# Batch 0's last scores masked on DVE, masks and products joined in pairs, and a new hand-written order, in a kernel of windowed attention and a gated long convolution

## Chip, cores and metric

One core of one Trainium2 chip. The metric is the device time of a launch in microseconds, the median of several runs. Engines: PE (matrix products), DVE (element-wise), ACT (exponentials, copies, casts), POOL (here it issues loads) and SP (issues stores and small copies).

## What is computed

Four batches, eight heads of 64, 768 positions. An attention in which a query sees the 96 keys up to its own position and the first 8 keys, with a bias that falls with distance, feeds a convolution over the whole length, done in frequency space between two gates:

```
keep   = is_global | is_local
scores = where(keep, q @ k.T / 8 - slope[h] * dist, -1e9)
a      = softmax(scores)
x      = (a @ v), heads side by side          # 4 x 768 x 512
x1, x2, x3 = split(x @ w_proj)
conv   = irfft(rfft(x2) * rfft(filter))
out    = (x1 * conv * x3) @ w_out
```

## The kernel before

The work of a batch goes through two halves. **Attention:** q and k rows are turned on PE (L703) and copied to `QT` and `KT` by ACT or DVE (L321). The keys are cut in seven blocks, in three groups, the thirds (`GRP`, `c` = 0, 1, 2); for each of four head pairs and each third a step `scores` (L737) makes 128x864 scores in two PSUM banks (L755), ACT takes their exponential into `E` (L770), and the bias and the window come in as a multiplication by `mask` on DVE (L787), a table of exponentials of the scaled distance tile `dg` that ACT makes head by head (L623; `dg` is shown as `eo` in the profile). In batch 0 the masks are not ready so early: while `c < NEAR` the step is a `near` one, where PE adds the bias by two matmuls of a scaled identity with `dg` (L749), and no multiplication follows. `values` (L805, L810) multiplies with v; DVE or ACT divide by the sums (L829, L833), and PE and a copy turn the result into `xT` (L851).

**Convolution:** `gate` (L931) makes x1 and x3 from `xT` and the outer columns of the projection `w`, ACT scales x1 and DVE multiplies (`g`, L945). `butterfly` (L860) makes sums and differences of `xT` so that the length-768 transform needs smaller products: `xab`, `xcf`, then `xo` and `xs`; in batch 0 it goes in two halves (head pairs 0 and 1), later in one. `proj` (L996) multiplies them with the middle columns of `w`, `fwd` (L1162) transforms, `products` (L1175) multiplies the spectrum `X` with the filter's two parts `h1` and `h2`, `inv` (L1027) and `mixed`, `gated` (from L1105) go back, and L1089 makes the output, which ACT or DVE copy out and SP stores.

**Order.** Nothing decides at build time: `ORDER` is a text with one word for each step, its number, its engine (P, A, V, G, S) and its PSUM banks; `i2b1` is two idle matmuls in bank 1. `Plan.schedule` reads it, and each engine runs its steps in that sequence. Where a step may run on ACT or DVE, the letter decides. All loads of q, k, v, `w` and the filter stand in POOL's sequence: `w` comes in five pieces (`WL`): columns 0, 1024, 256, 1280 (256 each) and 512 (512 columns, the projection's), each with the 128-row blocks side by side. The pieces 0 and 256 feed x1, 1024 and 1280 x3.

The words that the prediction uses: a *landing* is the arrival of a load; *xs* are the last differences of the butterfly (L886, L887), *xo* its odd part (L874).

## Time and profile before

| | before |
|---|---|
| median of 3 runs | 162.05 us (161.91 to 162.38) |
| profiled execution | 162.59 us |
| its span, first to last instruction | 160.8 us |
| mean clock of PE | 0.995 |
| loaded and stored | 21.95 MB, 136 GB/s on the mean |

The span is cut in views: busy time of each engine in a stretch (windows), the same instructions grouped by line (with mean duration and the idle time before them), the timeline of one engine (start, duration, line, operation, out<-in, count; in brackets the idle time before it and what ended it), the waits by who was waited for, the chain that ended last, and the loads with their time from issue to landing. PE stands for matmuls, PEld for its weight loads. Shapes are partitions x elements. In a row of the timeline several instructions of a kind are taken together, from the start of the first to the end of the last; start to start is an instruction's pace, which is shorter than its duration where two overlap.

### The profile page before, as it was taken

The page shows a single profiled execution, that of the slowest core. Times are in us where ns is not written, and L with a number is a line of the kernel's source. Part 1 is how long each engine was busy: PE and PEld are TensorE (multiplying, and loading weights), DVE is VectorE, ACT ScalarE, POOL GpSimd, SP SyncE. Part 2 cuts the span into 40 slices and gives each one's busy share as a digit, 9 for nine tenths or more (in the row PEclk, how much of TensorE's full clock was granted, in tenths as well). Part 3 has the DMA queues.
Part 4 walks back from the last instruction along what each step waited for, and adds up shares of the span by engine and source line. Part 5 has one row for each costly group of instructions (what it writes and reads, how often), then busy time and mean ns, then how long its engine had stood idle before and what let it go on. Part 6 is the DMA issues. An engine that isn't in the chain of part 4 may idle for free.

```text
span 160.8 us, 4208 instructions
## 1 busy us (share of the span) xinstructions
PE 151.4 (94%) x1587; PEld 91.8 (57%) x1587; DVE 150.3 (93%) x354; ACT 152.1 (95%) x299; POOL 77.1 (48%) x101
## 2 busy tenths in 40 slices
PE   5884999999999999999999999999999999999990
PEld 2543348745556678655567575545766754574540
DVE  5899989998999999999999999999999999999960
ACT  7999999999999999999999999999999999999761
POOL 7999469989988998989992000000000000000000
PEclk9999999999999999999999999999999999999998
DMA  5999999999999999999999985736002000330685
GB/s 165 212 178 166 154 149 132 135 161 163 186 166 152 147 131 136 164 151 155 153 103 152 134 158 102 71 131 248 17 33 104 0 0 0 132 135 0 264 325 196
DMA packets 84956, 21.95 MB, mean 136 GB/s; under 512 B 75584, under 2 KB 81992, under 8 KB 84936
## 3 DMA queue, kind: packets, MB, share of 16 engines
q0 software_dynamic: 73040, 12.11, 102.0%
q1 hardware_dynamic: 11896, 9.57, 22.4%
q8 instruction: 12, 0.20, 0.5%
q14 instruction: 8, 0.07, 0.1%
HBM read 25.40 MB, written 6.29 MB: 197 GB/s over the span
## 4 chain that ended last, share of the span: by engine, by line
PE 71%; ACT 11%; POOL 9%; DMA 3%; issue 3%; DVE 0%; POOLq 0%
PE bank L931 22%; PE bank L996 13%; PE bank L1089 13%; PE bank L755 4%; POOL qn L346 4%; POOL kn L346 4%; DMA w<-in_moe_w_proj_dram 3%; PE bank L1027 3%; PE bank L1162 3%; PE bank L805 3%; ACT E L770 3%; PE bank L851 3%; PE bank L810 3%; PE bank L703 2%; ACT mask L623 2%
## 5 line engine op out<-in xcount | busy, mean ns | idle before, releaser
L931 PE MATMUL bank<-xT,w 128*128 128x384 f16 x256 | 48.4, 326 | 0.3 <-DMA w<-in_moe_w_proj_dram 0.3
L770 ACT ACTIVATE E<-bank 128x864 f16<-128x864 f32 x48 | 41.7, 962 | 0.2 <-PE bank L755 0.2
L931 PEld LDWEIGHTS <-w 128*128 128x128 f16 x256 | 23.5, 98 | 16.7 <-DMA w<-in_moe_w_proj_dram 1.2
L346 POOL DMA_DIRECT2D vn<-in_v_dram x28 | 25.8, 936 | 1.6 <-DMA kn<-in_k_dram 0.8
L346 POOL DMA_DIRECT2D kn<-in_k_dram x25 | 21.5, 876 | 4.4 <-DVE eo L327 2.3
L1089 PE MATMUL bank<-wo,y 128*128 128x512 f16 (+1 forms) x100 | 23.2, 371 | 0.0
L346 POOL DMA_DIRECT2D qn<-in_q_dram x25 | 21.5, 870 | 1.6 <-PE bank L1034 0.5
L787 DVE TENSOR_TENSOR E<-E,mask 128x864 f16<-128x864 f16 x36 | 20.7, 600 | 0.0
L325 ACT ACTIVATE x<-bank 128x384 f16<-128x384 f32 x32 | 17.7, 579 | 1.0 <-PE bank L931 0.9
L325 ACT ACTIVATE ot<-bank 128x512 f32<-128x512 f32 (+1 forms) x23 | 14.9, 666 | 2.2 <-PE bank L1089 2.1
L996 PE MATMUL bank<-w,xs 128*128 128x512 f16 x64 | 16.0, 379 | 0.0
L805 PEld LDWEIGHTS <-E 128*128 128x128 f16 x224 | 14.1, 97 | 2.5 <-ACT E L770 0.2
L805 PE MATMUL bank<-vn,E 128*128 128x65 f16 x224 | 15.2, 193 | 0.0
L1089 PEld LDWEIGHTS <-y 128*128 128x128 f16 x100 | 9.4, 98 | 9.9 <-DVE y L1144 0.8
L810 PE MATMUL bank<-vn,E 128*128 128x65 f16 x192 | 15.0, 193 | 0.0
L321 ACT CAST ab<-bank 128x512 f16<-128x512 f32 x24 | 14.8, 658 | 0.0
L755 PE MATMUL bank<-QT,KT 64*128 64x216 f16 (+2 forms) x224 | 14.2, 242 | 0.5 <-DVE QT L321 0.4
L945 DVE TENSOR_TENSOR g<-bank,x 128x384 f16<-128x384 f32 x24 | 13.1, 548 | 0.9 <-PE bank L755 0.6
L810 PEld LDWEIGHTS <-E 128*128 128x128 f16 x192 | 13.2, 97 | 1.1
L755 PEld LDWEIGHTS <-KT 64*128 64x128 f16 x224 | 7.8, 94 | 10.4 <-issue 9.2
L829 DVE TENSOR_TENSOR xn<-bank,rc 128x512 f16<-128x512 f32 (+1 forms) x18 | 13.5, 761 | 0.1
L321 ACT CAST X<-bank 128x1024 f16<-128x1024 f32 x12 | 13.0, 1081 | 0.3 <-PE bank L1162 0.2
(155 smaller groups left out, 325.2 us busy)
## 6 DMA issues: line engine op xcount, KB each, us to landing
out_dram<-ot SPq DMA_DIRECT2D x23, 256.0 KB
vn<-in_v_dram POOLq DMA_DIRECT2D x28, 120.0 KB, 7.5
kn<-in_k_dram POOLq DMA_DIRECT2D x16, 96.0 KB, 5.1
qn<-in_q_dram POOLq DMA_DIRECT2D x16, 96.0 KB, 5.1
w<-in_moe_w_proj_dram POOLq DMA_DIRECT2D x4, 256.0 KB, 5.7
kn<-in_k_dram POOLq DMA_DIRECT2D x7, 120.0 KB, 6.8
g<-in_moe_filter_fft_dram POOLq DMA_DIRECT2D x1, 768.0 KB, 9.5
qn<-in_q_dram POOLq DMA_DIRECT2D x6, 128.0 KB, 7.2
```

The costliest lines, as they stand in the source:

```text
L321: {"A": nc.scalar.copy, "V": nc.vector.tensor_copy, "G": nc.gpsimd.tensor_copy}[e](out, in_)
L325: self.nc.scalar.mul(out, in_, c)
L346: return self.g.op(eng, 0.57 + 0.00035 * nbytes[0] if eng == "G" else 0.5, lambda _: e.dma_start(dst, src), w=w, r=r, nbytes=nbytes, name= ...
L755: nc.tensor.matmul(bs[hh].f32()[:, off:off + w], self.KT[hs, hp, P * m:P * m + P], self.QT[hs, hp, KL * m:KL * m + w], start=(off == 0 and ...
L770: g.op("A", act(864), lambda _: nc.scalar.activation(eo, bs[0].two()[:, :, 0:432].rearrange("p h (m w) -> p h m w", m=2), Act.Exp, scale=s ...
L787: g.op("V", dve(864, 2), lambda _: nc.vector.tensor_mul(eo, eo, mk), r=[("mask", 2 * hp), ("mask", 2 * hp + 1)], w=[("E", hp, gi)], name=" ...
L805: nc.tensor.matmul(o[:, n, hh], ef[:, at:at + P], vt[:, t, 2 * hp + hh, 0:D + 1], start=first, stop=(t == 0), skip_group_check=True)
L810: nc.tensor.matmul(o[:, n, hh], ef[:, at:at + P], vt[:, t - 1, 2 * hp + hh, 0:D + 1], start=False, stop=True, skip_group_check=True)
L829: nc.vector.tensor_mul(to, o[:, :, :, 0:D], rc.to_broadcast([P, 2, 2 * nt, D]))
L931: nc.tensor.matmul(bk.f32()[:, 0:h], self.w[:, c, o + P * j:o + P * j + P], self.xT[:, c, h * s:h * s + h], start=(c == 0), stop=(c == 3))
L996: nc.tensor.matmul(bk.f32(), src[:, c], w[:, c, DM:2 * DM], start=(c == 0), stop=(c == 3))
L1089: nc.tensor.matmul(bk.f32()[:, 0:n], y[:, c, P * t:P * t + P], self.wo[:, c, cs], start=(c == 0), stop=(c == 3))
```

## The change

Six things change. **Masks:** `PAIR_M` lists all batches and thirds, so one DVE instruction masks two head pairs (128x1728) where two did (128x864): 36 become 18 in batches 1 to 3. **Batch 0's last third:** `NEAR` is 2, so its four score steps lose their two bias matmuls each, and two joined masks are added. **Butterfly:** batch 0's comes in one instead of two halves (`JOIN0`), and the two instructions of the turned differences are one, in all batches. **Products:** the two with `h1` and `h2` are one instruction of 2048 elements (`h1`, `h2` in one tile; `X` has 8 slots, the last two are the old `p3`). **`neg`,** a table that nothing used, is not made. **Order:** a new `ORDER`, with other engine letters: from DVE to ACT go the copies and fills of `dg` (`second`), the scaling of `fold`, two fills of ones and one copy of `xT`; from ACT to DVE two casts of q and k, copies of `KT` and `QT`, two scalings of x1, one part of `xn` and three copies of outputs. Counts: DVE 356 to 310, ACT 301 to 297, PE 1587 to 1580 matmuls; POOL's 106 and SP's 53 stay, in the same sequence.

The code, and the first words of the two orders:

```diff
@@ -39,51 +39,50 @@
...
-44S 3G 1V 4V 46S 31G 5V 0V 21P5 55S 2A 29A 8V 48S 16P4 7V 22A 30V 11P2 54G 17A 23V 45A i2b1 53G 24V 12A 33V 6G 18V
-25A 19V 50G 82P1 47A 13V 32V 34G 20A 80P0 38A 51G 41A 26A 198P4 14V 52G 83A 36V 92P5 56V 71G 15A 204V 58S 200V 49V
...
+44S 3G 1V 4V 46S 31G 5V 0V 21P6 55S 2A 10V 29A 48S 11P1 9V 22A 33V 54G 7V 32A i1b0 23V 16P5 53G 45V i2b0 24V 6G 17A
+18A 47V 50G 82P4 12A 19V 80P6 40A 34G 13V 25A 51G 14V 37A 20A 36V 81A 52G 191P7 43V 35V 15A 49V 71G 56V 86P3 60G 57V
...
@@ -196,11 +195,13 @@
 
 class Fused:
     PERIOD = 40.0
-    NEAR = 3
+    NEAR = 2
     SPLIT = (3,4,5)
     SUMPE = ()
     TWICE = tuple((3,j,s) for j in range(4) for s in range(2))
-    PAIR_M = ()
+    PAIR_M = tuple((b,c) for b in range(4) for c in range(3))
+    JOIN0 = True
+    DIRECT = ()
     WARM = "sin"
     PAIR_G = ()
     PAIR_AB = ()
@@ -267,17 +268,17 @@
         self.fwd = t("fwd", [P, 8, P])
         self.fold = t("fold", [P, 4, P])
         self.inv = t("inv", [P, 4, P])
-        self.neg = t("neg", [P, 2, P])
+        self.neg = t("neg", [P, 2, P]) if self.SUMPE else None
         self.uw = t("uw", [P, 4, 2, 2, P])
         self.inr = t("inr", [P, 4, P])
-        self.p3 = t("p3", [P, 2, DM])
+        self.X = t("X", [P, 8, DM])
+        self.p3 = self.X[:, 6:8]
         self.twin = self.p3.rearrange("p a b -> p (a b)")[:, 0:512].rearrange("p (s a c) -> p s a c", s=2, a=2)
-        self.h1 = t("h1", [P, 4, DM])
-        self.h2 = t("h2", [P, 4, DM])
+        self.hh = t("hh", [P, 2, 4, DM])
+        self.h1, self.h2 = self.hh[:, 0], self.hh[:, 1]
         self.gt = [t(f"g{i}", [P, 4, S]) for i in range(2)]
         self.abp = t("ab", [P, 6, DM])
         self.ab = [self.abp[:, 3 * i:3 * i + 3] for i in range(2)]
-        self.X = t("X", [P, 6, DM])
         pp = t("pp", [P, 2, 4, DM])
         self.pp = pp
         self.p1, self.p2 = ([pp[:, x, 2 * i:2 * i + 2] for i in range(2)] for x in range(2))
@@ -569,9 +570,10 @@
                 f = self.fold[64 - 64 * (s % 2):P - 64 * (s % 2), (s + 2) % 4]
                 self.times(e, f, f, c * (1 - s // 2 * 2))
         g.op("AV", {"A": 4 * act(P), "V": 4 * dve(P, 4)}, scaled, w=[("fwd", 3), "foldp"], name="foldp")
-        g.op("AV", {"A": 2 * act(P), "V": dve(2 * P, 4)}, lambda e: [self.times(
-            e, self.neg[:, n], self.inv[:, 2 - 2 * n], -1.0) for n in range(2)] if e == "A" else self.times(
-            e, self.neg[:, ::-1], self.inv[:, 0:4:2], -1.0), r=[("inv", i) for i in range(7)], w=["neg"], name="neg")
+        if self.SUMPE:
+            g.op("AV", {"A": 2 * act(P), "V": dve(2 * P, 4)}, lambda e: [self.times(
+                e, self.neg[:, n], self.inv[:, 2 - 2 * n], -1.0) for n in range(2)] if e == "A" else self.times(
+                e, self.neg[:, ::-1], self.inv[:, 0:4:2], -1.0), r=[("inv", i) for i in range(7)], w=["neg"], name="neg")
 
     def distances(self):
 
@@ -881,11 +883,16 @@
         turned = xs.rearrange("p (a b) c m -> p a b c m", a=2)[:, ::-1, :, :, 64:P]
 
         def odd(_):
+            if n == 2:
+                ahead = xs.rearrange("p (a b) c m -> p a (b c) m", a=2)[:, ::-1, :, 64:P]
+                a, c = (x.rearrange("p (a b) c m -> p a (b c) m", a=2) for x in (right, left))
+                v.tensor_sub(ahead, a, c)
+                return
             for a in range(2):
                 ins = slice(2 * a, 2 * a + 2)
                 v.tensor_sub(turned[:, a], right[:, ins], left[:, ins])
         op(dve(512 * n, 2), lambda _: v.tensor_add(xs[:, :, :, 0:64], right, left), ("xr", "xc", "xf"), "xe")
-        op(2 * dve(256 * n, 2), odd, ("xr", "xc", "xf"), "xd")
+        op(dve(1024, 2) if n == 2 else 2 * dve(256, 2), odd, ("xr", "xc", "xf"), "xd")
 
     def gates(self, b, jp, s):
         nc, g, h = self.nc, self.g, self.S // 2
@@ -932,6 +939,12 @@
                                      self.xT[:, c, h * s:h * s + h], start=(c == 0), stop=(c == 3))
             g.op("P", pe(*[h] * 4), run, acq=[bk], r=xs + [("w", o // P + j)], name="gate")
             pts.append(bk)
+        if (b, j, s) in self.DIRECT:
+            x3, ko = gt[:, j, h * s:h * s + h], ("g", b % 2, j, s)
+            g.op("V", dve(h, 1, True), lambda _: nc.vector.scalar_tensor_tensor(
+                x3, pts[0].f32()[:, 0:h], X1_SCALE, pts[1].f32()[:, 0:h], op0=Alu.mult, op1=Alu.mult),
+                use=pts, w=[ko], name="g")
+            return
         x1, key = self.x1[self.turn4 % 4], ("x1", self.turn4 % 4)
         self.turn4 += 1
         g.op("AV", self.evac(h), lambda e: self.times(e, x1, pts[0].f32()[:, 0:h], X1_SCALE),
@@ -976,7 +989,7 @@
                     for j in (2 * jp, 2 * jp + 1):
                         self.gate(b, j, c - 1)
                 self.g.bias = 0.0
-        for js in ((0,), (1,)) if b == 0 else ((0, 1),):
+        for js in ((0,), (1,)) if b == 0 and not self.JOIN0 else ((0, 1),):
             self.butterfly(js)
 
 
@@ -1177,17 +1190,20 @@
         n, m = pair[0] // 2, len(pair) // 2
         xs = X[:, pair[0]:pair[0] + 2 * m]
         if n == 2:
-            g.op("V", dve(1024, 2), lambda _: nc.vector.tensor_mul(self.p3, xs, self.h2[:, 2:4]),
-                 r=[("h", s, 2) for s in pair],
-                 w=[("X", s) for s in pair], name="prod")
-            g.op("V", dve(1024, 2), lambda _: nc.vector.tensor_mul(xs, xs, self.h1[:, 2:4]),
-                 r=[("h", s, 1) for s in pair],
-                 w=[("X", s) for s in pair], name="prod")
+            to = X[:, 4:8].rearrange("p (x s) n -> p x s n", x=2)[:, ::-1]
+            g.op("V", dve(2048, 2), lambda _: nc.vector.tensor_mul(
+                to, xs[:, None].to_broadcast([P, 2, 2, DM]), self.hh[:, ::-1, 2:4]),
+                r=[("h", s, x) for s in pair for x in (1, 2)], w=[("X", s) for s in pair], name="prod")
             return
         p1, p2 = self.pp[:, 0, pair[0]:pair[0] + 2 * m], self.pp[:, 1, pair[0]:pair[0] + 2 * m]
         rs = [("X", s) for s in pair] + [("h", s) for s in pair]
         two = lambda x: x.rearrange("p (k c) n -> p k c n", c=2)
-        for to, h, key in ((p1, self.h1, "p1"), (p2, self.h2, "p2")):
+        if m == 1:
+            g.op("V", dve(2048, 2), lambda _: nc.vector.tensor_mul(
+                self.pp[:, :, pair[0]:pair[0] + 2], xs[:, None].to_broadcast([P, 2, 2, DM]),
+                self.hh[:, :, n:n + 1].to_broadcast([P, 2, 2, DM])),
+                r=rs, w=[("p1", n), ("p2", n)], name="prod")
+        for to, h, key in ((p1, self.h1, "p1"), (p2, self.h2, "p2")) if m > 1 else ():
             g.op("V", dve(1024 * m, 2), lambda _, to=to, h=h: nc.vector.tensor_mul(
                 two(to), two(xs), h[:, n:n + m, None].to_broadcast([P, m, 2, DM])),
                 r=rs, w=[(key, n + x) for x in range(m)], name="prod")
```

Three places in the order. First ACT, from the load of its exponential table to the first exponentials of batch 0 (`mask`, `E`), before:

```order
21 L623 ACT_TABLE_LOAD
22 L623 ACTIVATE mask<-eo 128x648 x2
23 L321 COPY QT<-bank_107 128x768
24 L770 ACTIVATE E<-bank_105 128x2x2x216
25 L770 ACTIVATE E<-bank_106 128x2x2x216
26 L321 COPY KT<-bank_107 128x6x120
27 L321 COPY KT<-bank_107 128x120
28 L321 COPY KT<-bank_107 128x7x6
29 L321 COPY KT<-bank_107 128x7x2
```

and with the change:

```order
20 L625 ACT_TABLE_LOAD
21 L625 ACTIVATE mask<-eo 128x648 x5
22 L326 ACTIVATE eo<-ident 128x128
23 L322 COPY QT<-bank_104 128x768
24 L322 COPY X<-fwd 128x512
25 L326 ACTIVATE eo<-ident 128x128
26 L625 ACTIVATE mask<-eo 128x648
27 L772 ACTIVATE E<-bank_104 128x2x2x216
28 L772 ACTIVATE E<-bank_105 128x2x2x216
29 L326 ACTIVATE eo<-ident 128x128
```

Six masks instead of two stand ahead of the first exponential, and the KT copies that lay between exponentials are gone from there.

Second DVE, the last steps of batch 0's butterfly (`xab`, `xcf`, `xo`, `xs`), among products of the gates (`g`) and masks of batch 1 (`E`), before:

```order
108 L787 TENSOR_TENSOR E<-E,mask 128x2x2x216
109 L878 TENSOR_TENSOR xcf<-xab,xcf 128x2x256
110 L787 TENSOR_TENSOR E<-E,mask 128x2x2x216
111 L887 TENSOR_TENSOR xs<-xcf 128x4x2x64
112 L787 TENSOR_TENSOR E<-E,mask 128x2x2x216
113 L945 TENSOR_TENSOR g_87<-bank_107,x_94 128x384 x2
114 L787 TENSOR_TENSOR E<-E,mask 128x2x2x216
115 L886 TENSOR_TENSOR xs<-xcf 128x2x2x64 x2
116 L787 TENSOR_TENSOR E<-E,mask 128x2x2x216 x6
```

and with the change:

```order
101 L958 TENSOR_TENSOR g_85<-bank_105,x_91 128x384
102 L894 TENSOR_TENSOR xs<-xcf 128x16x64
103 L784 TENSOR_TENSOR E<-E,mask 128x4x2x216
104 L328 TENSOR_SCALAR x_91<-bank_103 128x384
105 L958 TENSOR_TENSOR g_85<-bank_103,x_91 128x384
106 L889 TENSOR_TENSOR xs<-xcf 128x2x8x64
107 L958 TENSOR_TENSOR g_85<-bank_102,x_91 128x384
108 L784 TENSOR_TENSOR E<-E,mask 128x4x2x216 x3
```

The last `xs` (L886, now L889) is one instruction, directly behind the first of the last two `g`; before, both `g` and a mask stood ahead of it. Three masks follow.

Third DVE, the end of batch 1's masks, with the return from frequency space (`eo`, `mix`, `uw`) between, before:

```order
168 L1123 TENSOR_TENSOR eo<-eo,uw 128x8x128
169 L787 TENSOR_TENSOR E<-E,mask 128x2x2x216
170 L1124 TENSOR_TENSOR eo<-mix,uw 128x8x128
171 L787 TENSOR_TENSOR E<-E,mask 128x2x2x216
172 L945 TENSOR_TENSOR g_88<-bank_108,x_94 128x384
173 L787 TENSOR_TENSOR E<-E,mask 128x2x2x216
174 L1125 TENSOR_TENSOR eo<-mix,uw 128x8x128
175 L787 TENSOR_TENSOR E<-E,mask 128x2x2x216 x2
176 L834 RECIPROCAL rc_97<-bank_107 128x8
```

and with the change:

```order
149 L958 TENSOR_TENSOR g_86<-bank_103,x_91 128x384
150 L1134 TENSOR_TENSOR mix<-eo,uw 128x1024
151 L784 TENSOR_TENSOR E<-E,mask 128x4x2x216
152 L328 TENSOR_SCALAR uw<-uw 128x8x128
153 L958 TENSOR_TENSOR g_86<-bank_103,x_91 128x384
154 L1136 TENSOR_TENSOR eo<-eo,uw 128x8x128
155 L784 TENSOR_TENSOR E<-E,mask 128x4x2x216
156 L1137 TENSOR_TENSOR eo<-mix,uw 128x8x128
157 L784 TENSOR_TENSOR E<-E,mask 128x4x2x216
158 L958 TENSOR_TENSOR g_86<-bank_105,x_91 128x384
159 L1138 TENSOR_TENSOR eo<-mix,uw 128x8x128
```

Where five masks of one head pair stood among these steps, each handed over by itself, three joined ones stand.

More of the change, by code (lines that the diff above doesn't have):

```diff
@@ new lines @@
+502V 676A 660P3 804A 744V 753P45 677P67 661A 678P 754V 518P0 755V 665A 679A 499V 619P1 519A 666P23 807V 667P 750P67
+621A 682P45 668A 683P 751V 802V 813P01 684A 515P2 814V 500V 815A 620P3 752V 808P45 622V 772P67 669V 615P3 516A
+769P01 773V 680V 617A 517S 616P2 774A 520S 506P3 770V 618V 809V 771V 756P2 507A 757P 624P6 810V 758A 816P7 775P0
+670V 776P 817A 811P3 509P4 777A 685V 503P7 812A 681V 510A 695P01 839V 689P23 504A 696P 692P45 697A 693P 838V 690P
+779P7 691A 686P01 841V 687P 694A 784P2 840V 688A 819P3 842V 789P4 699V 843A 847P0 698V 781A 700V 793P1 791A 848A
@@ L87 @@
+714S 828P7 900V 711S 834P0 902V 830A 726S 914V 903P1 723S 836A 912V 719A 909P0 827V 904A 822V 720S 832V 837V 906P2
+905S 910A 913V 915V 911S 920P5 907V 921P 916P3 908S 922A 917P 923S 924P2 918A 925P 928P0 926V 929P 919S 930V 927S
+931S
 """
```

77 lines of the change are left out of this document (34 added, 43 removed).

## The prediction

> **What bounds the kernel now.** I read the page first, then the windows, the chain of waits, and last the stretch where the chain leaves PE. The page's engine line and its DMA line (tenths of busy time, 4 us a digit):
>
> ```profile
> PE 151.4 (94%) x1587; PEld 91.8 (57%) x1587; DVE 150.3 (93%) x354; ACT 152.1 (95%) x299; POOL 77.1 (48%) x101
> ...
> DMA  5999999999999999999999985736002000330685
> ```
>
> Three engines are over 90% busy, so the averages do not name the bound. The windows do (start and end, length, then busy time of PE, PEld, DVE, ACT and POOL, PE's clock, DMA share, GB/s):
>
> ```profile
> 40.00:43.50 3.50, 3.29 (x36) 2.07 (x33) 3.50 (x11) 3.50 (x8) 3.50 (x5) 1.00 1.47 181
> 43.50:46.30 2.80, 2.76 (x29) 1.72 (x30) 2.53 (x7) 2.58 (x5) 2.12 (x3) 1.00 1.86 169
> 46.30:80.00 33.70, 33.70 (x396) 22.08 (x393) 33.37 (x70) 33.18 (x57) 31.80 (x37) 1.00 2.14 151
> 80.00:150.00 70.00, 69.97 (x680) 42.66 (x679) 69.33 (x144) 69.47 (x154) 5.20 (x6) 1.00 0.66 88
> ```
>
> From 46.30 to 150.00 PE is busy 103.67 of 103.70 us at full clock. DVE and ACT are nearly as full, but PE does not wait for them. So the end is fixed by two things: when this solid stretch begins, and how much PE work is in it. The chain says what sets its beginning (start, length, what):
>
> ```profile
> 37.89 5.60 DMA w<-in_moe_w_proj_dram
> 43.54 2.12 PE bank L931 x12
> 45.66 0.67 PE bank L755 x16
> 46.33 2.70 PE bank L996 x12
> ...
> 151.70 5.41 PE bank L1089 x28
> ```
>
> A weight load is issued by POOL at 37.89 and lands at 43.49. The gates (L931) that need it start at 43.54, the first projection (L996) follows, and from there all is PE. The waits (who, for whom: sum, times, longest) and POOL's timeline add the rest:
>
> ```profile
> PEld L931 <- DMA w<-in_moe_w_proj_dram: 1.2, 3, 0.5
> ```
>
> ```profile
> 18.51 0.86 POOL L346 DMA_DIRECT2D kn<-in_k_dram  x1 [2.31 <-DVE eo L327]
> ...
> 21.59 1.64 POOL L346 DMA_DIRECT2D kn<-in_k_dram  x2 [1.39 <-ACT E L770]
> ...
> 37.89 1.52 POOL L346 DMA_DIRECT2D w<-in_moe_w_proj_dram  x2
> ```
>
> ```profile
> kn<-in_k_dram POOLq DMA_DIRECT2D x16, 96.0 KB, 5.1
> ...
> w<-in_moe_w_proj_dram POOLq DMA_DIRECT2D x4, 256.0 KB, 5.7
> ...
> w<-in_moe_w_proj_dram POOLq DMA_DIRECT2D x1, 512.0 KB, 7.5
> ```
>
> PE waited for w three times before 43.6, up to 0.5 us. The second load of the pair issued at 37.89 leaves half of 1.52 us later, at 38.65, takes 7.5 us and lands at about 46.1: the first projection needs just this one. **So two landings, 43.5 and 46.1, hold PE's start, and PE was at both within half a microsecond.** A load takes 5.6 us and more from issue to landing although POOL needs 0.8 us to issue one: they stand in a queue that moves data all the time (DMA is 9 in every slice from 4 to 96 us), and POOL's issues and their sequence are untouched by the change.
>
> **The change part by part.** *PE.* Batch 0's last third loses its bias matmuls, eight of 24:
>
> ```profile
> 16.31 0.54 PE L749 MATMUL bank<-eo 128*128 128x432 bf16 x2
> 16.78 0.36 PE L755 MATMUL bank<-QT,KT 64*128 64x216 f16 x4
> ```
>
> A pair of them costs 16.78 - 16.31 = 0.47 us, four pairs 1.9 us. All of it lies before 24 us, ahead of both landings. Between 43.5 and the first projection stand three gate groups and three score groups in both orders, and after it the same PE groups in another sequence (gates, projections, forward and inverse transforms, outputs, scores, values): nothing is taken out of the solid stretch. So the 1.9 us turn into waiting for w: worth 0. If that cover were gone they would be worth 1.9 us (first rival).
>
> *ACT.* It now makes six masks before its first exponential, where it made two:
>
> ```profile
> 11.38 1.38 ACT L623 ACTIVATE mask<-eo 128x648 f16<-128x648 bf16 x2
> 12.66 0.78 ACT L321 COPY QT<-bank 128x768 f16<-128x768 f16 x1
> 13.34 1.67 ACT L770 ACTIVATE E<-bank 128x864 f16<-128x864 f32 x2
> ...
> 19.62 5.66 ACT L770 ACTIVATE E<-bank 128x864 f16<-128x864 f32 x7
> 25.12 1.42 ACT L623 ACTIVATE mask<-eo 128x648 f16<-128x648 bf16 x2
> ```
>
> ```profile
> L321 ACT CAST kn<-h 128x768 f16<-128x768 f32 x1 | 0.8, 834 | 0.0
> ...
> L321 DVE COPY eo<-eo 128x216 bf16<-128x216 bf16 x1 | 0.4, 405 | 0.0
> ```
>
> A mask costs (12.66 - 11.38)/2 = 0.64 us, an exponential (25.12 - 19.62)/7 = 0.79. Four more masks ahead are 2.6 us; the two copies and four fills of the distance tile that DVE gives up I put at 1.2 us on ACT (three times the 0.4 of the larger copy; 0.4 to 2.4 if the fills cost nothing or each as much); two input casts (0.8 each) and a KT copy with its parts (0.9, row below) go to DVE, 2.5 us less. That is +1.3; with two more small scalings ahead I put the first exponential 1.3 to 2 us later, at about 15. In batch 0 this is paid back: twelve exponentials then run almost without a mask between, and end near 25 (15 + 12 x 0.79 and a scaling), against 25.1 with two masks fewer done. Up to the last KT copy, on which the last scores before the gates hang, my count of ACT's work ahead is even (casts, two KT copies, one x1 out; fills, a mask, one xT copy, a ones fill in):
>
> ```profile
> 41.20 1.09 ACT L321 COPY KT<-bank 128x720 f16<-128x720 f16 x3
> ```
>
> ```profile
> 42.54 0.75 PE L755 MATMUL bank<-QT,KT 64*128 64x216 f16 x12
> ```
>
> That copy ends at 42.1 now; the last scores run to about 43.2. Even if it came 0.3 us later, PE would be at the gates by 43.5. Value 0, bounds -0.1 and, if my count is 2.5 us short, +1.3.
>
> *DVE.* The prices of joining come from these groups (mean ns of one behind the comma):
>
> ```profile
> L787 DVE TENSOR_TENSOR E<-E,mask 128x864 f16<-128x864 f16 x36 | 20.7, 600 | 0.0
> ...
> L1191 DVE TENSOR_TENSOR pp<-X,h 128x1024 f16<-128x1024 f16 x16 | 10.5, 672 | 0.0
> ...
> L872 DVE TENSOR_TENSOR xcf<-xab 128x1024 f16<-128x1024 f16 x3 | 2.1, 687 | 0.0
> ...
> L872 DVE TENSOR_TENSOR xcf<-xab 128x512 f16<-128x512 f16 x2 | 0.8, 418 | 0.0
> ```
>
> 512 elements more cost 687 - 418 = 269 ns, so 864 more cost 454 and a joined mask lasts about 1.05 us. Successive ones overlap by 80 ns (two 864 masks: 1.12 us together, row at 79.17 below, not 1.20), so a fixed part of 0.07 us per instruction is saved. Masks: 36 x 0.52 = 18.7 becomes 20 x 0.97 = 19.4 us (two of them new), +0.7. Products: 12 instructions fewer, -0.8. Butterflies and differences: nine joins, -0.6; `neg` gone, -0.2. The copies and fills that change engine nearly cancel. DVE's total moves by less than half a microsecond. What counts here are the last differences of batch 0 (`xs`). Before, the first projection takes `xo`, made long ahead; in the new order it takes `xs`, and on DVE these differences stand right behind the product `g` of the first gates that the landing at 43.5 lets go:
>
> ```profile
> 44.47 1.14 DVE L945 TENSOR_TENSOR g<-bank,x 128x384 f16<-128x384 f32 x2 [0.24 <-PE bank L931]
> 45.52 0.60 DVE L787 TENSOR_TENSOR E<-E,mask 128x864 f16<-128x864 f16 x1
> 46.04 0.49 DVE L886 TENSOR_TENSOR xs<-xcf 128x256 f16<-128x256 f16 x2
> ```
>
> DVE waits for these gates already (the bracket: 0.24 us). The product starts at 44.47 in both; half of 45.52 - 44.47 is 0.5, and with 0.69 for the joined differences they are ready at 45.7, where PE's landing asks for them at 46.1 to 46.3. Value 0 with 0.5 us to spare; and they are done 0.8 us sooner than before (46.04 + 0.49), a lead that DVE carries on.
>
> One place does get tighter. A joined mask delivers both its halves only at its end, 0.45 us after the first was ready before. Where PE takes the masked scores of batch 1's last rows:
>
> ```profile
> 79.17 1.12 DVE L787 TENSOR_TENSOR E<-E,mask 128x864 f16<-128x864 f16 x2
> ```
>
> ```profile
> 80.02 0.22 PE L805 MATMUL bank<-vn,E 128*128 128x65 f16 x2
> ```
>
> the first of these masks ends at 79.77 and PE reads at 80.02, 0.25 us later. In the new order one projection, one values group and two forward groups fewer stand ahead of that values group, by their paces 1.7 us, and DVE has 0.8 us less to do between the differences and this mask. With the lead of 0.8 that leaves 0.25 + 0.8 + 0.8 - 1.7 = 0.15 us to spare; without it PE stalls 0.65: bounds 0 and +0.65. I take +0.1, since DVE was idle only 33.70 - 33.37 = 0.3 us in this stretch, so that a lead is used.
>
> *Tail.* The last outputs, 28 matmuls from 151.70, and ACT's last eviction are the same; their y products come some tenths earlier on DVE. Value 0, bounds -0.2 and +0.1.
>
> **Sum.** 43.5 (landing) + 2.8 (gates and scores to the first projection) + 110.8 (PE to 157.1) + 3.7 (last eviction, output load) = 160.8, the span, and 1.8 around it make the profiled execution's 162.59. The terms of the change: 0 (PE) + 0 (ACT) + 0 (DVE) + 0.1 (masks) + 0 (tail) = +0.1, profiled 162.7. The median of the runs is 0.54 below the profiled execution; I carry the same offset: 162.1.
>
> A row that speaks on how firmly the landing stands:
>
> ```profile
> 9.90 6.30 POOL L346 DMA_DIRECT2D vn<-in_v_dram  x7
> ...
> 40.19 4.57 POOL L346 DMA_DIRECT2D vn<-in_v_dram  x5
> ```
>
> An issue of vn took 6.30/7 = 0.90 us at 10 us, while DVE scales and copies tables, and 4.57/5 = 0.91 us at 40 us, beside masks and butterflies: DVE work with two inputs slows POOL by 0.01 us an issue, about. [...]
>
> **Rivals.** *The saving comes through.* POOL's waits of 2.31 and 1.39 us are put down to DVE and ACT. If they are real engine waits, a shorter start could let the w loads go earlier by as much as PE saves, 1.9 us at most and 1.6 likely: 160.5. Against it: the loads behind them took 5.6 us in the queue, so an earlier issue lengthens the queue, not the landing. 8%. *ACT is late.* Six masks and the fills ahead of the first exponential could delay batch 0's whole start, so that the last KT copy ends after 43.2 instead of 42.1; from there each microsecond moves the gates, and so the end, one for one. With my count 2.5 us short: +1.2, 163.3, slower. For it: ACT is 95% busy. Against: its work ahead is even, and batch 0 runs at the exponentials' pace in both. 13%. *The joined masks are late.* DVE loses its lead of 0.8 us at 46 (it waits for scores that come when they came before), and the handover near 80 costs 0.65 us, perhaps once more later: 162.6 to 163.2. 16%. *POOL is held.* If each of some ten joined instructions before 38 us held an issue for its extra 0.27 to 0.45 us, the loads would leave 3 us late, of which 0.5 (5.6 less the 5.1 of a small kn load) is queue: 164.7. 3%. *Joining loses the rate*: broadcast operands in the joined products or masks run at half speed, +1 us for each of 12 or 20, 170 or more. 2%.
>
> **How the numbers follow.** Forecast 58%, in 161.6 to 162.5. The range runs from 161.3 (part of the saving) to 163.2 (late masks, ACT a little late); outside remain the full saving, most of the late ACT, and the two last rivals, about 2 in 10. A measurement of this kernel can tell about 0.3%, 0.5 us. Faster by more: 8% from the first rival and 5% from landings or tail earlier than I see, 13%. Slower by more: 13 of ACT, 10 of the masks' 16, 3 and 2, 28%. Within: 59%.
>
> **What would show it.** Right: the changed profile has PE waiting for w at the gates near 43.5 for 1 us or more, w landings within 0.3 us of 43.5 and 46.1, PE solid from 46.3 on, and PE's total 1.5 us smaller. First rival: w lands at 42 or earlier. Late ACT: the gates of 43.5 start later and wait for scores' banks or KT. Late masks: PE idle before L805 near 78, released by DVE. POOL: w issued after 39. Lost rate: joined masks over 1.2 us. Wrong altogether would be a new PE wait between 46 and 157 of which I name no cause.

## The result: slower, by about one per cent

| | before | changed |
|---|---|---|
| median | 161.98 us (161.90 to 162.38, 4 runs) | 164.45 us (163.68 to 165.36, 4 runs) |
| ratio | 1 | 1.0136 [1.0105, 1.0168] |
| again, beside e9 and e10 on one chip | 162.27 us (23 runs) | 163.59 us (163.18 to 164.07, 8 runs), ratio 1.0074 [1.0045, 1.0103] |
| profiled execution, span | 162.59, 160.8 us | 164.56, 162.8 us |
| mean granted clock of PE, profiled execution | 0.995 | 0.977 |

Ratios leave out a run that took over 1.5% longer than the fastest of the same kernel on that chip, which struck one of the 23 above and one of the six of e12. The forecast was no change (162.1, 161.3 to 163.2). It was wrong: the changed kernel was 1.4% slower in the first measurement and 0.7% in the second. The profile says where: not in the solid stretch that the prediction watched, but in the first 20 us, and at PE's clock. What the kernel before lacks to a clock of 1 lies behind its last matmul, where the record falls to half at 159.3 us, so a reading of 0.995 need not mean a loss during the work.

### The profile page after: what moved, and what is told of

Same layout as the page of the kernel before. It is cut to its first block, busy times and chain, and to the rows that moved or that the text cites. A ratio compares the mean times of both kernels' runs of the same rounds, so it can differ in the third digit from the quotient of the medians.

```text
span 162.8 us, 4153 instructions
## 1 busy us (share of the span) xinstructions
PE 151.7 (93%) x1580; PEld 93.1 (57%) x1580; DVE 151.6 (93%) x308; ACT 151.9 (93%) x295; POOL 77.0 (47%) x101
## 4 chain that ended last, share of the span: by engine, by line
PE 72%; DVE 8%; ACT 8%; DMA 4%; issue 3%; POOL 3%; POOLq 0%; DVEq 0%; ACTq 0%
PE bank L938 22%; PE bank L1102 13%; PE bank L1009 10%; PE bank L757 5%; ACT E L772 5%; DMA kn<-in_k_dram 4%; PE bank L1040 3%; PE bank L853 3%; PE bank L807 3%; PE bank L812 3%; PE bank L1175 2%; PE bank L705 2%; PE bank L751 1%; DVE xn L831 1%; PE bank L708 1%
## 5 line engine op out<-in xcount | busy, mean ns | idle before, releaser
L1102 PE MATMUL bank<-wo,y 128*128 128x512 f16 (+1 forms) x100 | 22.7, 370 | 0.0
L784 DVE TENSOR_TENSOR E<-E,mask 128x1728 f16<-128x1728 f16 x20 | 20.8, 1047 | 0.3 <-ACT mask L625 0.3
L326 ACT ACTIVATE x<-bank 128x384 f16<-128x384 f32 x30 | 16.1, 557 | 0.8 <-PE bank L938 0.6
L326 ACT ACTIVATE ot<-bank 128x512 f32<-128x512 f32 x22 | 13.7, 666 | 1.7 <-PE bank L1102 1.4
L831 DVE TENSOR_TENSOR xn<-bank,rc 128x512 f16<-128x512 f32 (+1 forms) x19 | 14.3, 767 | 0.2
L757 PE MATMUL bank<-QT,KT 64*128 64x216 f16 (+2 forms) x224 | 13.7, 246 | 0.3 <-ACT E L772 0.2
```

The lines of the kernel that those rows point to most:

```text
L326: self.nc.scalar.mul(out, in_, c)
L757: nc.tensor.matmul(bs[hh].f32()[:, off:off + w], self.KT[hs, hp, P * m:P * m + P], self.QT[hs, hp, KL * m:KL * m + w], start=(off == 0 and ...
L784: g.op("V", dve(1728, 2), lambda _: nc.vector.tensor_mul(ep, ep, mk), r=[("mask", h) for h in range(hs.start, hs.stop)], w=[("E", hp - 1, ...
L831: nc.vector.tensor_mul(to, o[:, :, :, 0:D], rc.to_broadcast([P, 2, 2 * nt, D]))
L1102: nc.tensor.matmul(bk.f32()[:, 0:n], y[:, c, P * t:P * t + P], self.wo[:, c, cs], start=(c == 0), stop=(c == 3))
```

## The profile after

The engine line and PE's granted clock in tenths, 4.07 us a digit:

```profile
PE 151.7 (93%) x1580; PEld 93.1 (57%) x1580; DVE 151.6 (93%) x308; ACT 151.9 (93%) x295; POOL 77.0 (47%) x101
...
PEclk9995799999999999999999999999999999999999
```

Two digits are not 9: between 12 and 20 us PE ran at 5 and 7 tenths of full clock. PE is busy as long as before (151.7 against 151.4) although it lost eight bias matmuls: what it saved it spent again at the lower clock. The windows of that place (columns as in the prediction, PE's clock third from the end):

```profile
10.00:12.00 2.00, 0.25 (x10) 0.09 (x4) 1.97 (x9) 1.99 (x4) 2.00 (x3) 0.95 1.04 151
12.00:14.00 2.00, 0.60 (x12) 0.60 (x14) 2.00 (x10) 2.00 (x5) 2.00 (x3) 0.50 1.01 150
14.00:16.00 2.00, 2.00 (x32) 1.42 (x28) 1.37 (x5) 1.80 (x4) 2.00 (x3) 0.50 1.13 169
16.00:18.00 2.00, 2.00 (x12) 0.40 (x10) 2.00 (x3) 0.89 (x1) 0.03 (x1) 0.50 1.57 185
18.00:20.00 2.00, 1.55 (x20) 0.81 (x19) 1.87 (x10) 1.81 (x4) 0.49 (x1) 0.84 2.32 145
```

PE does almost nothing from 10.3 to 13.4 us, the clock goes to half, and when work comes PE runs it at half speed. PE's timeline says what it waited for:

```profile
9.72 0.53 PE L708 MATMUL bank<-ident,kn 128*64 128x128 f16 x12
13.40 0.85 PE L708 MATMUL bank<-ident,kn 128*64 128x128 f16 x12 [3.15 <-DMA kn<-in_k_dram]
14.04 1.49 PE L708 MATMUL bank<-ident,qn 128*64 128x128 f16 x24
15.47 0.90 PE L751 MATMUL bank<-eo 128*128 128x432 bf16 x2
16.30 0.54 PE L757 MATMUL bank<-QT,KT 64*128 64x216 f16 x4
```

The new order has a group that turns k (L708, the k group from here on) ahead of the first scores. Its load is issued at 7.43 and lands at 13.36:

```profile
7.43 5.93 DMA kn<-in_k_dram
...
13.40 2.13 PE bank L708 x36
```

In the old order two score steps and a q turn stood ahead of the group that turns this k, so PE idled only 1.60 us, at full clock. Now the first scores begin at 15.47 instead of 9.97, and at half speed a pair of bias matmuls lasts 16.30 - 15.47 = 0.83 us, where the prediction's rows had 0.47. ACT, which the prediction feared would be late, waits for PE:

```profile
16.88 0.89 ACT L772 ACTIVATE E<-bank 128x864 f16<-128x864 f32 x1 [1.09 <-PE bank L757]
18.19 0.89 ACT L772 ACTIVATE E<-bank 128x864 f16<-128x864 f32 x1 [0.42 <-PE bank L757]
```

From there the delay runs to the end. The gates that answer to the 43.54 of before start at 45.23, the projection that answers to 46.26 at 48.03:

```profile
45.23 2.12 PE L938 MATMUL bank<-xT,w 128*128 128x384 f16 x12
47.28 0.73 PE L757 MATMUL bank<-QT,KT 64*128 64x216 f16 x12
48.03 1.04 PE L1009 MATMUL bank<-w,xs 128*128 128x512 f16 x4
```

No bracket stands there: PE does not wait for w any more; it is late on its own. And behind the first projection nothing happens:

```profile
48.00:158.00 110.00, 109.83 (x1104) 67.94 (x1103) 107.41 (x195) 106.30 (x213) 34.59 (x40) 1.00 1.05 118
```

PE is busy 109.83 of 110 us at full clock. From the first projection to the end of the last matmul it is 110.84 us before and 110.80 after. Of the 2.0 us that the span grew, 1.77 are there at the first projection.

The key times of all kernels, from their traces (us, of one profiled execution each): the start of batch 0's first exponential and the end of its last, then the start of the gates for the w pieces 0 and 1280 and of the first projection. The last column is the median of all runs; those of e1 to e4, e5 to e8 and e9 to e11 were taken on one chip each, and on these chips the kernel before had medians of 162.54, 162.18 and 162.27 (162.24 beside e12):

| kernel | first exponential starts | last one ends | gates w(0) | gates w(1280) | first projection | median |
|---|---|---|---|---|---|---|
| before | 13.34 | 25.28 | 31.83 | 43.54 | 46.26 | 161.98 |
| changed | 16.88 | 27.77 | 34.88 | 45.23 | 48.03 | 164.45 |
| e1 | 15.71 | 26.00 | 33.11 | 43.24 | 45.99 | 162.63 |
| e2 | 15.72 | 26.01 | 33.29 | 43.42 | 46.17 | 162.56 |
| e3 | 15.72 | 26.79 | 33.90 | 44.03 | 46.78 | 163.62 |
| e4 | 15.71 | 26.28 | 33.43 | 43.57 | 46.32 | 162.75 |
| e5 | 15.82 | 29.03 | 35.29 | 46.59 | 49.31 | 165.97 |
| e6 | 15.24 | 27.94 | 34.20 | 45.50 | 48.23 | 164.34 |
| e7 | 15.71 | 25.98 | 33.10 | 43.55 | 46.43 | 164.01 |
| e8 | 14.44 | 26.25 | 34.86 | 44.89 | 47.62 | 163.95 |
| e9 | 15.70 | 25.98 | 33.30 | 43.43 | 47.11 | 162.63 |
| e10 | 15.71 | 26.26 | 33.38 | 43.52 | 46.27 | 162.56 |
| e11 | 16.21 | 27.38 | 34.49 | 44.85 | 47.66 | 163.59 |
| e12 | 15.70 | 25.98 | 33.10 | 43.23 | 45.98 | 163.93 |

## The experiments

The theory to be tested, CLOCK: the wait for the k load itself costs little, since ACT has masks to make until 15.8 us anyway; what costs is that PE's clock stood at 0.50 when the work came. Rivals: LOAD, PE is late because k comes late; ACT, six masks ahead of the first exponential make batch 0 late.

**e1, idle matmuls in the wait.** (90 is the k group that waits, 41 the DVE step ahead of it in the text, `i10b1` ten unused matmuls in bank 1.)

```diff
-... 192V 195V 41V 90P1 95V 76A ...
+... 192V 195V 41V i10b1 90P1 95V 76A ...
```

> The changed kernel with ten idle matmuls (result unused) put on PE into its 3.15 us wait for the k load, ahead of the k group that waits; the load, its landing at about 13.4 us and all other work stay. Theory CLOCK (the wait itself costs little, since ACT is at its masks until 15.7 us anyway; what costs is the lower clock granted to PE after it idled): granted clock back to 0.99 or more, the 36 turning matmuls behind the wait in 1.45 us instead of 2.07, first exponential at about 15.8 instead of 16.9, the gates for w(0) at 32.5 instead of 34.9, time 162.2 (161.6 to 162.9). Theory LOAD (PE late because k comes late): no change, 164.2 to 164.6. Theory ACT (six masks ahead of the first exponential make batch 0 late): 164 or a little less, the exponentials' end unmoved at 27.5.

Measured: 162.63 us (162.31 to 162.89, 10 runs), ratio to before 1.0007 [0.9985, 1.0029], clock 1.00. PE's timeline:

```profile
10.93 2.46 PE L318 MATMUL bank<-uw 128*128 128x512 f16 x10
13.32 0.53 PE L708 MATMUL bank<-ident,kn 128*64 128x128 f16 x12
13.68 1.17 PE L708 MATMUL bank<-ident,qn 128*64 128x128 f16 x24
14.79 0.54 PE L751 MATMUL bank<-eo 128*128 128x432 bf16 x2
15.26 0.36 PE L757 MATMUL bank<-QT,KT 64*128 64x216 f16 x4
```

```profile
12.00:14.00 2.00, 2.00 (x31) 1.10 (x29) 2.00 (x10) 2.00 (x5) 2.00 (x3) 1.00 1.13 112
14.00:16.00 2.00, 1.85 (x28) 0.72 (x22) 2.00 (x6) 2.00 (x5) 2.00 (x3) 1.00 1.15 189
```

The k group starts at 13.32, as late as in the changed kernel, but the 36 turns behind it take 14.79 - 13.32 = 1.47 us instead of 15.47 - 13.40 = 2.07, and the bias pair 0.47 instead of 0.83. The idle matmuls hold the group until then, since its load had landed at 12.08 in this execution. So the work starts as late as in the changed kernel and only its speed differs, and the slowdown is gone: LOAD falls, and so does ACT, whose six masks are still there. The changed kernel was not measured beside e1; beside e9 it was, on one chip, and there 163.59 us became 162.63 with two idle matmuls and nothing else.

**e2, four idle matmuls** (`i4b1` in the same place).

> The same with four idle matmuls, which leave some 2 us of PE idle before the k group. Theory CLOCK, with a limit on how long PE may idle: the profile of before shows PE idle 1.60 us at about the same place with no loss of clock, so 2 us may still be free: about 162.2 as with ten; if any gap counts in proportion, half the loss, 163.2. Theories LOAD and ACT: 164 or more, as with ten.

Measured: 162.56 us (162.32 to 163.04), ratio 1.0002 [0.9980, 1.0024], clock 1.00; 1.08 us of idle time are left ahead of the k group. Filling most of the gap is as good as filling it all.

**e3, the first scores ahead of the k group.**

```diff
-... 41V 90P1 95V 76A 63G 42A 84P0 93A 61G 87V 88P2 26A 96P45 38A ... 120A 153P45 ...
+... 41V 96P01 90P4 95V 76A 63G 42A 84P2 93A 61G 87V 88P7 26A 38A ... 120A 153P01 ...
```

> The changed kernel with the first score step of batch 0 moved ahead of the k group that waits for its load (banks of four steps exchanged for it, nothing else): PE has work at 11.9 us and its longest idle time falls to about 1.6 us. Theory CLOCK: clock 0.99, first exponential at 15.7, right behind ACT's sixth mask, time 161.6 to 162.6. Theory LOAD: part of the loss back, since the first scores no longer stand behind the load, 163 to 164. Theory ACT: 164 or more, as the first exponential still stands behind six masks.

Measured: 163.62 us (162.79 to 164.41), ratio 1.0063 [1.0033, 1.0093], clock 0.986. A miss: the gap was cut, but the clock fell all the same, only later. In PE's timeline, and in windows of 3.3 to 3.4 us:

```profile
13.67 0.53 PE L708 MATMUL bank<-ident,qn 128*64 128x128 f16 x12 [0.37 <-DMA qn<-in_q_dram]
15.87 0.53 PE L751 MATMUL bank<-eo 128*128 128x432 bf16 x2 [1.67 <-DVE QT L322]
```

```profile
13.50:16.80 3.30, 1.41 (x19) 0.83 (x20) 3.30 (x10) 3.16 (x8) 2.54 (x3) 1.00 1.19 192
16.80:20.20 3.40, 3.13 (x26) 1.47 (x27) 2.77 (x10) 3.14 (x5) 0.73 (x1) 0.50 2.15 153
20.20:23.60 3.40, 3.40 (x44) 1.57 (x41) 2.71 (x6) 3.36 (x5) 3.40 (x6) 0.99 2.40 151
```

No gap here is longer than 1.67 us, but PE is busy only 1.41 of 3.30 us, and the next 3.40 us run at half clock. So in this execution the fall needed no long gap: ahead of it stood little work, 1.41 us in 3.30.

By its median alone e3 would fit LOAD (163 to 164). Its ten runs, which all execute the same kernel, say otherwise, for their times follow the clock on record:

| mean granted clock of the run | runs | time |
|---|---|---|
| 0.999 | 1 | 162.79 us |
| 0.986 to 0.989 | 5 | 163.10 to 163.67 us |
| 0.977 to 0.978 | 4 | 164.13 to 164.41 us |

One stretch of 3.41 us at half clock takes 1.1% off the mean clock (1.7 of 161.3 us), so the rows fit runs with no such stretch, with one and with two, at about 0.7 us each; the profiled run, at 0.986, has one. The one run without a lost stretch lies within the range of e1.

**e4, the bias matmuls back** (the masks on DVE stay).

```diff
+        biased = near or (self.b == 0 and gi == 2)
-            if near:
+            if biased:
```

> e1_idle10 with the eight bias matmuls of batch 0's last third put back on PE, while the masks on DVE stay, so the bias comes in twice in this third and the output is another. It prices what the change takes off PE. If PE's start is held by the landings of w or by ACT's exponentials, as the prediction had it: 0 to +0.3 us against e1_idle10. If PE is late on its own work up to 45 us: up to +1.9 us.

Measured: 162.75 us (162.52 to 163.59), ratio 1.0023 [0.9998, 1.0047]; the gates for w(1280) at 43.57 instead of e1's 43.24. Taking 1.9 us of matmuls off PE ahead of 24 us is worth 0.1 us by the medians, which is within the noise, and 0.3 us at the gates.

**e5 and e6, the same gap in the kernel before,** bare and filled. If the clock is the cause, it must do the same there.

```diff
-86P7 37A 10V 62G 39V 96P01 203V ... 73A 84P6 64G ... 93A 113P23 63G ... 42V 97A 90P4 87V 61G 94P5 114A
+86P7 37A 10V 62G 39V 203V ... 73A 64G ... 93A 63G ... 42V 90P4 96P01 97A 87V 61G 94P5 84P6 113P23 114A
 (e6: 86P7 i11b2 37A ...)
```

> The kernel before, with its first two score steps and one q turn of batch 0 moved behind the k group that waits for its load and its bank; nothing else. PE then idles from about 10.0 to 13.3 us, as long as in the changed kernel. Theory CLOCK: the granted clock falls to half for one or two stretches of 3.4 us in the profile, mean clock 0.97 to 0.985, time 163.5 to 165. Theory ORDER (the rest of the change makes it slow, a gap alone does not): 162 to 162.8 with the clock at 0.99 or more.

> e5_before_gap with eleven idle matmuls in that gap. Theory CLOCK: clock 0.99 or more and 162.0 to 162.9; what is left over the kernel before is the price of the later first exponential (about 14.4 us instead of 13.3). Theory ORDER: no difference from e5_before_gap.

Measured: e5 165.97 us (165.58 to 166.23), ratio 1.0232 [1.0186, 1.0278]; e6 164.34 us (164.22 to 164.63), ratio 1.0128 [1.0089, 1.0168]. Filling the gap is worth 1.6 us here too, on one chip, so CLOCK holds in the other kernel. Both are misses by their level (163.5 to 165 and 162.0 to 162.9 were expected): here the wait itself costs 2 us, since the kernel before makes only two masks first and ACT then has to wait for scores, as its timeline in e6 shows:

```profile
12.63 0.78 ACT L321 COPY QT<-bank 128x768 f16<-128x768 f16 x1
15.24 0.89 ACT L770 ACTIVATE E<-bank 128x864 f16<-128x864 f32 x1 [1.82 <-PE bank L755]
```

In e5 the view of the profile shows a granted clock of 1.00 throughout, yet matmuls behind the gap ran at half speed until about 16.9:

```profile
13.62 0.85 PE L706 MATMUL bank<-ident,kn 128*64 128x128 f16 x12 [3.25 <-DVE inr L327]
14.40 0.90 PE L749 MATMUL bank<-eo 128*128 128x432 bf16 x2
```

The duration (0.90 where 0.54 is usual for such a pair) is the safer witness. The trace's record of the clock holds changes only, and in e5 its first one is a rise to full clock at 16.80 us; what lies ahead of it is shown as 1.00. The matmuls ahead of the gap were slow too (twelve turns at 8.17 us took 0.85 us, where 0.53 is usual). So in this execution the clock did not fall: PE came to the gap at half speed and had not reached full clock yet; in e6 the first rise came at 12.34 us. The mean clock of a run misses such a late rise, which would explain why two runs of e5 read 0.999 and 1.00 and took as long as the two at 0.979.

**e7, masks and products cut again** (each joined step issues two instructions; here the mask).

```diff
-                g.op("V", dve(1728, 2), lambda _: nc.vector.tensor_mul(ep, ep, mk),
+                g.op("V", dve(1728, 2), lambda _: [nc.vector.tensor_mul(
+                    ep[:, n:n + 2], ep[:, n:n + 2], mk[:, n:n + 2]) for n in (0, 2)],
```

> e1_idle10 with the joined masks and products cut into two instructions again, in the same place and step: 32 DVE instructions more, some 0.067 us each, 2.1 us of DVE work in all, 0.3 of it ahead of 46 us. Theory HIDDEN (as predicted, DVE's savings are worth nothing, since PE is the bound and DVE keeps up): 0 to +0.3 us against e1_idle10. Theory DVE BOUND (DVE keeps up only because of the joins): +1 to +2 us, with PE waits released by DVE between 46 and 157.

Measured: 164.01 us (163.63 to 164.92), ratio 1.0117 [1.0079, 1.0155], against e1's 1.0007. The theory HIDDEN fails. (The two were measured on different chips; the ratios to the kernel before differ by 1.1%, the medians by 1.4 us.) The groups of the changed kernel, and then of e7, price one instruction:

```profile
L784 DVE TENSOR_TENSOR E<-E,mask 128x1728 f16<-128x1728 f16 x20 | 20.8, 1047 | 0.3 <-ACT mask L625 0.3
```

```profile
L784 DVE TENSOR_TENSOR E<-E,mask 128x864 f16<-128x864 f16 x40 | 22.1, 598 | 0.0
```

and among the waits of PE's weight loads two on DVE are longer in e7 than in e1, which has 0.5 and 0.2 us in these rows:

```profile
PEld L1103 <- DVE y L1158: 0.9, 2, 0.5
...
PEld L1010 <- DVE xs L890: 0.7, 2, 0.4
```

In the trace, the first projection is 0.44 us later than in e1, and from there to the end of the last matmul 111.92 us pass instead of 110.77: of some 2.1 us of DVE work 1.6 reached the end in these two executions. So in the new order DVE has next to no time to spare. Whether it had more in the kernel before was not tried.

**e8 and e10, an earlier first exponential.** Both are e3 with idle matmuls in its two gaps; e8 also moves two masks behind batch 0's exponentials. (96 is the first score step.)

```diff
-... 41V 96P01 90P4 95V ... 89V 119P67 ... 
+... 41V 96P01 i4b4 90P4 95V ... 89V i5b6 119P67 ...
 (e8 also: 75A and 74A, two masks, from ahead of the first exponential to behind 118A, the last one of batch 0)
```

> e3_scores_first with idle matmuls in the two gaps that are left (four and five) and two of the six masks moved behind batch 0's exponentials. If PE is held by ACT's first exponential (15.7 us in e1 to e3), it comes at 14.4, the gates for w(0) run at 32.0 instead of 33.1, the gates for w(1280) wait for the landing at 42.8, and the first projection runs at 45.4 to 45.6: 161.3 to 161.9, some 0.3% under the kernel before. If the PE work between the gates holds it instead: as e1_idle10, 162.3 to 162.7.

> e8_best without its moved masks: the first score step ahead of the k group, idle matmuls in both gaps, all six masks ahead of the first exponential as in the changed kernel. Theory MASKS (e8 lost because the two masks that ACT makes later delay its copies of the filter's spectrum, on which PE waited 1.07 us at 27): back to the time of e1_idle10, 162.3 to 162.7, with the gates for w(0) at 33. Theory SCORES (the changed sequence of turns and scores on PE makes e8 late): as e8, 163.8 to 164.2.

Measured: e8 163.95 us (163.85 to 164.19), ratio 1.0104 [1.0070, 1.0139]; e10 162.56 us (162.39 to 163.15), ratio 1.0015 [0.9985, 1.0045]. The two masks are the only difference of the two, 1.4 us (on two chips; 0.9% by the ratios). In e8 the first exponential came at 14.44, as hoped, but the last at 26.25, as without: between them ACT waited 1.41 us for scores. Then the masks stood ahead of ACT's copies of the filter's spectrum, and PE waited for them:

```profile
26.04 1.46 ACT L625 ACTIVATE mask<-eo 128x648 f16<-128x648 bf16 x2
27.30 0.68 ACT L326 ACTIVATE hh<-bank 128x512 f16<-128x512 f32 x1
```

```profile
28.04 0.38 PE L688 MATMUL bank<-pp,fwd 128*128 128x512 f16 x1 [1.06 <-ACT hh L326]
```

Of these two places for the two masks, the one ahead of the first exponential is the better: there they fill a time in which ACT would wait.

**e9 and e11, two idle matmuls, and the changed kernel again on the same chip.**

> The changed kernel with only two idle matmuls ahead of the k group that waits, which leaves PE idle for some 2.2 us of the 3.15 (1.1 us with four, where the clock held). If the loss of clock needs a gap of most of 3 us: full clock and the time of e2_idle4, 162.6. If a gap counts together with the thin work around it (in e3 a gap of 1.67 us was enough): clock at half for one or two stretches of 3.4 us in some runs, 163.2 to 164.4 and a wide spread.

> The changed kernel as it is, beside the other two on one chip: 163.7 to 165.4, clock 0.97 to 0.98, so that the differences of e9 and e10 to it hold on this chip too.

Measured: e9 162.63 us (162.41 to 163.78), ratio 1.0033 [1.0005, 1.0062], clock 0.996; e11 163.59 us (163.18 to 164.07), ratio 1.0074 [1.0045, 1.0103], clock 0.979. Two idle matmuls do most of it: e9's profile has gaps of 0.79 and 1.43 us with the clock at 1.00 through them. Two of its ten runs took 163.6 and 163.8 us. The first is the profiled one: its second w landing came at 46.97 and PE waited for it, with no clock lost. The other has a mean clock of 0.984, as the runs of e3 with one slow stretch had, so a lost stretch is likely there; it has no trace. e11 is slightly under its expected range, and its eight runs read 0.978 to 0.999.

**e12, w earlier.** On e1 (69 and 70 issue the last two pieces of w, 430 and 237 a load of q and one of v):

```diff
-... 68G 430G 237G ... 69G ... 70G ...
+... 68G ... 69G 70G 430G 237G ...
```

> e1_idle10 with the last two pieces of w issued ahead of two other loads (one of q, one of v) instead of behind them: they should land some 1.3 us earlier, at 41.5 and 44.1 us. Theory LANDING (the landings of w hold PE's start, as the prediction had it): the first projection up to 0.6 us earlier and 162.0. Theory OWN WORK (with the clock mended PE comes to these gates at 43.2 on its own work, 0.5 us behind the landing): the gates and the first projection stay within 0.2 us of e1_idle10's 43.2 and 46.0, time 162.3 to 162.8. Against: if PE waits for the delayed load of q, up to 1 us more.

Measured: 163.93 us (163.21 to 166.21, 6 runs), ratio 1.0084 [1.0057, 1.0110], over the expected range. The two pieces landed at 41.57 and 44.08 instead of 42.75 and 45.42; the gates and the projection did not move (43.23 and 45.98 against 43.24 and 45.99). PE was there on its own work. The time is worse because the delayed v load was needed soon after:

```profile
51.51 0.22 PE L807 MATMUL bank<-vn,E 128*128 128x65 f16 x2 [2.76 <-DMA vn<-in_v_dram]
```

No version beat the kernel before: e1, e2 and e10 are level with it.

## Why the prediction was wrong

*What failed.* The step on ACT: "Even if it came 0.3 us later, PE would be at the gates by 43.5", and with it "the first exponential ... at about 15", the last to end "near 25". They came at 16.88 and 27.77, and the sum's first term, PE at the gates with the landing at 43.5, became 45.23 with no wait for w. I counted the work ahead on ACT and took PE as ready, because its own work ahead was 1.9 us less. I did not walk PE's own first 20 us in the new order, where a group waits for a load that was known, from the trace of before, to land at about 12.5; and no term of the sum allowed for PE's clock to fall. The experiments put the loss on the clock: with the wait kept and the clock held, 1.0136 became 1.0007 (e1), and on one chip 1.0074 became 1.0033 (e9). None of the signs named for a right forecast came: no wait for w at those gates, and PE's total grew by 0.3 us where it was to shrink by 1.5. In the changed kernel's trace half clock lasted 6.83 us, twice 3.41, and began 1.6 us after PE's last matmul; the last section has the rows.

*PE's saving worth nothing.* Right in size (e4: 0.1 to 0.3 us of 1.9), but by luck, since its reason was wrong. I took the landings of w for the cover. They are not: in e1, with the clock mended, PE comes to those gates 0.5 us after the landing, and in e12 an earlier landing moves nothing (43.23 against 43.24). The cover lies in batch 0 itself: its last exponential ends at 26.0 to 26.3 in e1, e2, e4, e8 and e10, whether the bias is there (e4) or the first exponential comes 1.3 us earlier (e8). That ACT's exponentials and the copies ahead of the scores pace it is argued from these times; no run varied them alone.

*The solid stretch.* Right: 110.84 and 110.80 us, and no new wait of PE's matmuls in it.

*Joining on DVE.* The durations were right (1047 ns for 1.05 us; 1220 ns, L1194, for a product of 2048 elements in place of two of 670 and 686 ns). "Value 0" held for all that the change does on DVE together, since with the clock mended the kernel is level with the one before (e1), but not for the joins: e7 prices those of masks and products at 1.1% (1.0117 against 1.0007). The two came out even by luck. DVE was busy 150.3 us beside PE's 151.4 in the kernel before, between 46 and 150 us PE's matmuls did not wait for it, and I read that as slack. Its total was to move by less than half a microsecond; it grew by 1.3 to 151.6 us in spite of the joins, since the new order takes casts, KT and x1 copies from ACT, and without the joins DVE is late.

*The handover near 79 us.* Allowed +0.1, up to +0.65; there was no wait of PE. The joined mask ends at 80.41 and PE reads at 80.66, as close as before (0.25 us).

*The landings.* Said to be within 0.3 us of 43.5 and 46.1; they came at 42.75 and 45.35. POOL issued the first of these two loads at 37.11 instead of 37.89, and the landing moved by as much (5.64 us from issue to landing against 5.60): so an earlier issue did not just lengthen the queue, as I had argued against the first rival. The first rival's gain still came through in no run, for PE was not held by these landings any more. (The DMA line of before has its 9s up to 92 us, not 96; nothing hangs on it.)

*The rivals.* "ACT is late" had the direction and nearly the place (the gates of 43.5 late) but not the cause: ACT was idle, 1.09 and 0.42 us, for PE. Its price of 163.3 was for 1.2 us; the gates were 1.7 us late. "POOL is held" took each joined instruction to hold an issue for its extra 0.27 to 0.45 us; no run shows such a hold. The w load was issued at 37.11 us, not after 39, and an issue of vn took 6.36/7 = 0.91 us from 9.68 on and 4.68/5 = 0.94 us from 39.42 on, where it had taken 0.90 and 0.91.

*What stays open.* Why the loss was 1.4% in one measurement and 0.7% in the other is not settled. The two profiled executions lost the same 6.83 us of clock; in e11's the k load landed 0.7 us earlier, and its gates for w(0) came at 34.49 instead of 34.88, which accounts for part. Over all runs the mean clock was 0.969 to 0.978 in the first and 0.978 to 0.999 in e11, and such readings miss a late first rise (e5). That the change without its loss of clock is neither better nor worse than the kernel before is shown (e1, e2, e10); which of its moves would be worth something on their own is not.

## What to carry to other kernels

Walk the busiest engine's own queue first, load by load, when an order changes: a group that waits for a load holds all that stands behind it on its engine (3.15 us in the changed kernel), however much work was taken off. A thin stretch of PE could cost twice here, once as waiting (2 us in e6, nothing to be seen in e1) and again as half speed (the next 3.4 us in e3, 6.8 in the changed kernel); idle matmuls in such a wait gave back 0.4% (e9), 1.0% (e6) and 1.3% (e1). An engine that makes no one wait need not have time to spare: try it by putting work back (1.1% in e7). And where one kernel's runs differ, set their times beside their clocks (e3).

## What the runs showed of the hardware

In the changed kernel PE went idle at 10.25 us; the granted clock, full until 11.8, was at half by 12.0 and came back at 18.6:

```profile
11.60:11.80 0.20, 0.00 (x0) 0.00 (x0) 0.20 (x4) 0.20 (x2) 0.20 (x1) 1.00 1.05 158
11.80:12.00 0.20, 0.00 (x0) 0.00 (x0) 0.20 (x3) 0.20 (x1) 0.20 (x1) 0.54 1.06 161
18.40:18.60 0.20, 0.20 (x2) 0.00 (x0) 0.20 (x4) 0.20 (x1) 0.00 (x0) 0.50 2.14 138
18.60:18.80 0.20, 0.20 (x2) 0.00 (x0) 0.20 (x1) 0.20 (x1) 0.00 (x0) 0.89 2.26 138
```

That is 1.6 us after PE's last matmul, and 6.8 us of half clock, two stretches of 3.4; e3 had one, and lost the clock with PE busy 1.41 of the 3.30 us ahead.

*Where a limit may lie.* The changes of the clock lie a multiple of 3.41 us apart (8.40, 11.82 and 18.64 us in the changed kernel; 9.15 and 159.3 us, 44 times as long, in the kernel before), so these traces can be cut into stretches of this length at their changes. PE was busy for this long of the 3.41 us:

| kernel | stretch | PE busy | then |
|---|---|---|---|
| e11 | 8.50 to 11.91 | 1.41 us | clock falls |
| e3 | 13.41 to 16.83 | 1.44 us | clock falls |
| changed | 8.40 to 11.82 | 1.64 us | clock falls |
| before | 12.56 to 15.97 | 1.72 us | clock stays |
| e9 | 10.25 to 13.66 | 1.84 us | clock stays |
| e10 | 8.55 to 11.97 | 2.01 us | clock stays |

In these six executions the clock fell after 1.64 us of work or less and stayed after 1.72 or more. A limit between the two, about half of the stretch, is an estimate from this table, whose busy times rest on modelled ends of matmuls. At half clock, 1.83 us (changed, from 11.82) and 2.59 us (e11, from 11.91) did not bring the full clock back; 3.14 us (e3, from 16.83) did. By that estimate the kernel before, with 1.72 us in the stretch of its own 1.60 us wait, is close to the limit.

*The start was slow.* Twelve turns took 0.85 us ahead of the first rise on record and 0.53 behind it in the kernel before, six took 0.80 and 0.51 us in the changed one. That rise came at 9.15 and 8.40 us in these two, between 8.50 and 12.34 in the other executions, and at 16.80 in e5.
